# Parts of x for three batches and of LN's rows for two groups, made in token rows and transposed by DMA

## The chip, the cores and the metric

One core of a Trainium2 chip runs the whole program. The metric is the device time of one execution in microseconds; of the kernel before it is 833.95 us, the median of three runs (833.41 to 834.34). The engines go by these names: PE is TensorE (PEld its weight loads), DVE is VectorE, ACT is ScalarE, POOL is GpSimd, SP is SyncE, which here only issues DMAs.

## The reference

Three blocks in a row, all in f32: attention with a threshold, a LayerNorm with an MLP, and a token mixing with a channel product.

```python
scores = q @ k.T / sqrt(64)                 # 4 batches, 8 heads, 576 tokens
scores = where(scores >= max - tau, scores, -1e9)
x = softmax(scores) @ v                     # -> x: 4 x 576 x 512
xn = (x - mean) / sqrt(var + 1e-6) * g_ln
x = x + relu(xn @ w_ch1) @ w_ch2            # 512 -> 2048 -> 512
theta = x @ w_theta
y = w_tok_r @ (x*cos(theta)) + w_tok_i @ (x*sin(theta))   # over the tokens
u = x + y
out = u + relu(u @ w_ch)
```

## The kernel before

**Two parts for every operand.** The large products are made in fp16 with three products each: an f32 operand is scaled, rounded to fp16 (the rounded part, `hi`), and what is left of it is stored as a second fp16 (the difference, `lo`); rounded x rounded, rounded x difference and difference x rounded are added in PSUM.

**Who sets the order.** Nothing is ordered by hand. Each step is an `op(...)` with the operations it depends on, the buffers it acquires and releases (`Slot` of a `Res`) and a table of costs by engine (T for TensorE, A, V, G, Q for SP's queue). `Plan.run` plays the list several times, ranks the steps by their latest start and writes out one fixed order for each engine; TensorE goes by a `key`. A step with several engines in its table is given to the one that the plan sees finish first. A step that takes or frees another buffer can so move neighbours on all engines.

**Stages.** The attention runs to about 423 us, with LN and a first part of the MLP ("A") mixed in; the rest of the MLP ("B", products `p1_B...` and `c_...`) runs to about 630 us, and from 591 us on the token-mixing block goes batch by batch. Tokens come in row tiles of 128. Batches 0 and 1 are a pair of nine tiles, `xl_0_0` to `xl_0_8` (the tile in the middle, `xl_0_4`, holds 64 tokens of each batch and is called the tail), batches 2 and 3 a second pair, `xl_1_0` to `xl_1_8`. These tiles live in `x` slots and are loaded by SP from DRAM (L1349).

**LN.** For one row tile of a group (three tiles): `norm` writes the normalized rows `xn` in f32; `trans` (L1163) transposes them on TensorE, four blocks of 128 x 128 into PSUM; `hi` (L296 or L298, ScalarE or VectorE) rounds them from PSUM into `ringX`; `lo` (L309, VectorE) writes the difference. `ringX` then feeds the products of the MLP.

**The token-mixing block, for each batch b.**
- `scales` (L1457): TensorE makes `px_p` for the pair p from sums of squares; VectorE and GpSimd make a power of two of it (L619, L622, L625), the scale of x for theta, and small constants in `cs` (L1460 to L1475).
- `transposes(b)`, quoted below: the four transposes of a tile of x on TensorE (L1525, `pt3_...`), `hi` on ScalarE with the scale (L304), `lo` on VectorE (L1547), into `x1Tb`, which holds x transposed, rounded part and difference. The tail goes into a buffer of `hbuf`, and `tail1` and `tail2` copy its halves into the two batches' `x1T`.
- `thetas(b)`: 12 matmuls of 512 columns for a tile (L1573), then the reduction of theta on ScalarE, VectorE and GpSimd (L1591 to L1597).
- `make_z(b)`: sine, cosine (ScalarE), two products with x (L1660, VectorE), and the two parts of z (L298 to L309); the tail's are stacked first (L1694, L1695).
- `mix(b)`: y, 54 matmuls of 288 columns for each of four column blocks (L1737); the order of the rows of z ends with the tail's. Then u = x + y from PSUM (L1759), with the difference of x added (`post`, L1764, VectorE or GpSimd), and the parts of u written back over `x1Tb` (L304, L1770).
- `chan(b)`: o, 24 matmuls of 288 columns for each of four column blocks (L1795), each reading all four blocks of `x1Tb`; then relu, sum and the store.

`th_0` can only start when `x1T0` is there, `mix(0)` when all of z is. SP issues its DMAs in the order of its queue: one whose data are not ready holds up those behind it. The attention already turns its probabilities with DMA transposes on this queue (L1042, 108 of them, nine blocks of 128 x 128 each, `PT<-ringP`).

Of the kernel before, what the change touches and what calls it, by code (L numbers as in the profile page):

```python
# [75 lines left out]
MT = 2  # L76
IDLE = 200.0
NTINY = 960
BUSY = 0.7
LATE = 25000.0  # L80
CX = [0, 760.0, 1250.0]
CHA, CHV, CHG = [0, 680.0, 1160.0], [0, 690.0, 1290.0], [0, 758.0, 1370.0]
CLV, CLG = [0, 930.0, 1600.0], [0, 1206.0, 2060.0]
# [187 lines left out]
def tile_kernel(  # L271
# [45 lines left out]
    def vc(n, x=1.04):  # L317
        return 157.0 + x * n
# [10 lines left out]
    def gc(n):  # L329
        return 145.0 + GC * n  # L330
# [20 lines left out]
    rY = Res("y", 0)  # L351
    rXs = Res("x", NXS)
    rN = Res("xn", 2)
    rG = Res("g", 8)
    rR = Res("raw", NRAW)
    rQ, rK = Res("q", NQ), Res("k", NK)
# [102 lines left out]
    op(warmup, [k_ones], (warm,), (warm,), T=4000, key=-1e9)  # L459


    def cvt(src, shape, hi, lo, name, start=(), acq=(), kind="cvt", peak=None, late=None, early=False):


# [6 lines left out]
        def s0(e):  # L471
            if early:
                raw = rawe[sl.i // 2][:, sl.i % 2]
            else:
                raw = (lp if sl.i < NRAW else later["wb"]).tile([128, 512, 2], I32, tag=str(sl), name=f"raw_{name}")
# [626 lines left out]
    def ln_group(p, gi, base):  # L1102
# [44 lines left out]
        for t in range(nt):  # L1147
            sn, ms = Slot(rN), Slot(rM)

            def norm(e, t=t, sn=sn):  # L1150
                rs = st["rs"]
                st["xn", t] = lp.tile([128, S], F32, tag=str(sn), name=f"xn_{nm}_{t}")[:, 0:512]
                if e is A:
                    A.activation(out=st["xn", t], in_=x[p, t0 + t], func=AF.Identity,
                                 bias=rs[:, 1, t:t + 1], scale=rs[:, 0, t:t + 1])
                else:
                    V.tensor_scalar(out=st["xn", t], in0=x[p, t0 + t], scalar1=rs[:, 0, t:t + 1],
                                    scalar2=rs[:, 1, t:t + 1], op0=ALU.mult, op1=ALU.add)

            def trans(e, t=t, ms=ms):  # L1160
                st["pt", t] = m_tile(ms, [128, KB, 128], f"ptr_{nm}_{t}")
                for c in range(KB):
                    T.transpose(st["pt", t][:, c, :], st["xn", t][:, c * 128:(c + 1) * 128], ident)  # L1163

            def hi(e, t=t):
                st["xt"] = ringX[:, sx.i]
                copy(e, st["xt"][:, :, 0, t * 128:(t + 1) * 128], st["pt", t])

            def lo(e, t=t):
                cs = slice(t * 128, (t + 1) * 128)  # L1170
                sub(V, st["xt"][:, :, 1, cs], st["pt", t], st["xt"][:, :, 0, cs])

# [325 lines left out]
    def transposes(b):  # L1498
        p, odd = b // 2, b % 2
        sl = Slot(rY)  # L1500
        st = x1T[b] = {"sl": sl, "ops": [], "c": {}}
        t0 = 5 if odd else 0
        key = nkey() if b else KEY0

        def alloc():
            if "t" not in st:
                y = later["yp"].tile([128, KB, 2, S], F16, tag=str(sl), name=f"x1T{b}")
                st["t"] = [y[:, :, a] for a in range(2)]
            return st["t"]

        for t in range(5):
            if t == 4 and odd:
                def tail2(e):
                    for a in range(2):
                        copy(e, alloc()[a][:, :, 512:576], tails[p]["t"][:, :, a, 64:128])
                st["ops"].append(op(tail2, [tails[p]["op"]] + st["ops"][:1], (), (tails[p]["sl"],),
                                    A=2 * ac(256), V=2 * vc(256, .95)))
                continue
            ms = Slot(rM)
            ss = {}  # L1520

            def tr(e, t=t, ms=ms, ss=ss):
                ss["pt"] = m_tile(ms, [128, KB, 128], f"pt3_{b}_{t}")
                for c in range(KB):
                    T.transpose(ss["pt"][:, c, :], x[p, t0 + t][:, c * 128:(c + 1) * 128], ident)  # L1525

            acq = [ms]
            if t == 0:
                acq.append(sl)
            if t == 4:  # L1530
                tails[p] = {"sl": Slot(rG, 3)}
                acq.append(tails[p]["sl"])
            o = st["tr"] = op(tr, [xf[p, t0 + t], sx_ops[p], st.get("tr")], acq, (x_slot[p, t0 + t],), T=460, key=key + 0.01 * t)

            def dst(a, t=t):
                if t < 4:
                    return alloc()[a][:, :, t * 128:(t + 1) * 128]
# [12 lines left out]
            o = op(lo, [o], (), (ms,), V=690, kind="ev")  # L1550
            if t < 4:
                st["ops"].append(o)
            else:
                tails[p]["op"] = o

                def tail1(e):
                    for a in range(2):
                        copy(e, alloc()[a][:, :, 512:576], tails[p]["t"][:, :, a, 0:64])
# [363 lines left out]
```

## Time and profile before

| | us |
|---|---|
| median of 3 runs | 833.95 (833.41 to 834.34) |
| profiled execution | 833.26 |
| its span (first to last instruction) | 831.5 |
| PE busy | 821.0 (99%) |
| DVE busy | 621.0 (75%) |
| ACT busy | 535.0 (64%) |
| POOL busy | 355.8 (43%) |

The mean granted clock of TensorE is 0.999 of full speed. The span leaves out 1.8 us of the execution's own time, before the first and after the last instruction. Busy times are sums over an engine's instructions; they don't tell which engine is waited for at a given place, for that there are the rows of waits and of the timeline, where the idle time ahead of an instruction stands in square brackets with the instruction that ended it. A busy time in the timeline covers a matmul's drain, so the pace of matmuls is read from the start of one group to the start of the next.

### The profile page before, as it was taken

Reading aid. Unit: us, or ns where it says so; the run is one execution under the profiler, and the core shown is the slowest. Engines: PE = TensorE matmul, PEld = TensorE weight load, DVE = VectorE, ACT = ScalarE, POOL = GpSimd, SP = SyncE. Lnnn points to the kernel's source line nnn. Section 1 sums busy time; section 2 is a strip of 40 time slices with the busy share of each in tenths; the row PEclk is TensorE's granted clock in tenths of the full one; section 3 lists DMA queues with packets and bytes.
Section 4 is the critical chain, followed back from the end, with each engine's and each line's share of the span. In section 5 each row is a group of like instructions: output and inputs, shape, how many; then the busy total and the mean of one; then the engine's idle time right before and its main releaser. Section 6 shows DMA issues by size and latency. Waiting matters only on the chain. (4 is left out here: it accounts for less than half of the span.)

```text
span 831.5 us, 17300 instructions
## 1 busy us (share of the span) xinstructions
PE 821.0 (99%) x6625; PEld 543.4 (65%) x6625; DVE 621.0 (75%) x1279; ACT 535.0 (64%) x987; POOL 355.8 (43%) x444
## 2 busy tenths in 40 slices
PE   9999999999999999999999999999999999999997
PEld 8888866655566576666565555555555777667776
DVE  4878799999687887787557756766577693799943
ACT  5899999999588788888535543554476351564602
POOL 1332478787285465656321212221153250465611
PEclk9999999999999999999999999999999999999999
DMA  8433699894579799697563421744033010010011
GB/s 230 143 99 122 196 207 170 187 208 97 122 132 206 137 233 184 119 165 141 131 168 94 169 94 48 249 162 177 1 97 120 27 46 13 1 44 15 16 43 58
DMA packets 173235, 101.20 MB, mean 122 GB/s; under 512 B 136289, under 2 KB 154209, under 8 KB 173153
## 3 DMA queue, kind: packets, MB, share of 16 engines
q1 hardware_dynamic: 172864, 100.10, 49.5%
q8 instruction: 52, 0.85, 0.4%
q14 instruction: 31, 0.25, 0.1%
q10 hardware_dynamic: 288, 0.00, 0.0%
HBM read 52.50 MB, written 15.73 MB: 82 GB/s over the span
## 5 line engine op out<-in xcount | busy, mean ns | idle before, releaser
L701 PEld LDWEIGHTS <-w 128*128 128x128 f16 x1152 | 110.5, 98 | 80.7 <-issue 7.3
L701 PE MATMUL p_A<-ringX,w 128*128 128x384 f16 x864 | 149.9, 326 | 0.0
L724 PE MATMUL chA<-w,hbuf 128*128 128x512 f16 x648 | 149.2, 379 | 0.0
L724 PEld LDWEIGHTS <-hbuf 128*128 128x128 f16 x864 | 82.5, 99 | 93.6 <-issue 5.4
L979 DVE TENSOR_SCALAR_CACHE_REDUCE ringE<-S,ncoef 128x576 f32<-128x576 f32 x144 | 112.7, 812 | 27.2 <-PE S L878 21.1
L309 POOL TENSOR_TENSOR ringP<-ringE,ringP 128x512 f16<-128x512 f32 (+2 forms) x110 | 109.2, 1004 | 21.0 <-ACT ringP L296 16.1
L995 ACT ACTIVATE ringE<-ringE,tiny 128x576 f32<-128x576 f32 x144 | 105.5, 770 | 2.0 <-POOL tiny L987 1.0
L878 PE MATMUL S<-kf,qf 64*128 64x288 f32 (+1 forms) x576 | 98.5, 426 | 0.0
L1737 PE MATMUL y<-tok,z 128*128 128x288 f16 x768 | 97.2, 286 | 0.0
L1737 PEld LDWEIGHTS <-z 128*128 128x128 f16 x768 | 75.1, 98 | 19.2
L1021 ACT ACTIVATE ringE<-ringE,ntaup 128x576 f32<-128x576 f32 x108 | 78.6, 764 | 0.1
L707 ACT ACTIVATE hbuf<-p_A 128x384 f16<-128x384 f32 x72 | 35.2, 488 | 63.1 <-PE p_A L701 62.6
L878 PEld LDWEIGHTS S<-kf,qf 64*128 64x128 f32 (+1 forms) x576 | 56.9, 186 | 19.5 <-issue 4.5
L906 PEld LDWEIGHTS <-PT 128*128 128x128 f16 (+1 forms) x1680 | 57.3, 100 | 12.8 <-issue 5.4
L300 POOL TENSOR_SCALAR ringP<-ringE 128x576 f16<-128x576 f32 x63 | 44.7, 712 | 36.8 <-ACT ringE L1021 30.4
L906 PE MATMUL pv<-va,PT 128*128 128x65 f16 (+3 forms) x1680 | 60.2, 193 | 0.0
L1213 DVE SCALAR_TENSOR_TENSOR x<-chA,qs,x 128x512 f32<-128x512 f32 x54 | 40.3, 747 | 25.5 <-PE chA L724 25.3
L710 DVE SCALAR_TENSOR_TENSOR hbuf<-p_A,hbuf 128x384 f16<-128x384 f32 x72 | 39.6, 551 | 22.7 <-ACT hbuf L707 22.2
L724 PE MATMUL c<-w,hbuf 128*128 128x512 f16 x216 | 51.0, 379 | 0.0
L701 PE MATMUL p_B<-ringX,w 128*128 128x384 f16 x288 | 50.7, 326 | 0.0
L1795 PE MATMUL o<-x1T,cw 128*128 128x288 f16 x384 | 48.0, 286 | 1.3 <-DVE x1T L1770 1.3
L309 DVE TENSOR_TENSOR ringP<-ringE,ringP 128x512 f16<-128x512 f32 (+2 forms) x58 | 44.0, 768 | 2.9 <-ACT ringP L296 1.4
(228 smaller groups left out, 1392.8 us busy)
## 6 DMA issues: line engine op xcount, KB each, us to landing
raw_w<-in_w SPq DMA_DIRECT2D x20, 512.0 KB, 4.5
rawe<-in_w SPq DMA_DIRECT2D x12, 512.0 KB, 4.8
raw_tok<-in_wtok SPq DMA_DIRECT2D x12, 432.0 KB, 4.4
qf<-in_qT SPq DMA_DIRECT2D x20, 256.0 KB, 3.5
kf<-in_kT SPq DMA_DIRECT2D x16, 288.0 KB, 4.0
xscr<-x SPq DMA_DIRECT2D x18, 256.0 KB, 2.4
xl<-xscr SPq DMA_DIRECT2D x18, 256.0 KB, 5.1
out<-uo SPq DMA_DIRECT2D x16, 288.0 KB, 2.1
```

The lines of the kernel that those rows point to most:

```text
L300: G.tensor_scalar(out=out, in0=in_, scalar1=1.0, scalar2=0.0, op0=ALU.mult, op1=ALU.add)
L309: e.tensor_tensor(out=out, in0=a, in1=b, op=ALU.subtract)
L701: T.matmul(st["ps"][:, :n], lhsT=ch.w1(a, c), rhs=xt()[:, c, bb, :n], start=(kk == 0), stop=(kk == 11))
L724: T.matmul(ps, lhsT=h[:, a, t * 128:(t + 1) * 128], rhs=ch.w2(bb), start=(first and (a, bb) == M2[0]), stop=(stop and (a, bb) == M2[2]))
L878: T.matmul(w["S"][:, n, 0:288], lhsT=qd.q["f"][r, hp], rhs=d.k["f"][r, n * 288:(n + 1) * 288], start=True, stop=True)
L906: T.matmul(out[:, j * 65:j * 65 + n], lhsT=l, rhs=r[:, j * 65:j * 65 + n], start=(k == 0), stop=(k == len(seq) - 1))
L979: V.tensor_scalar(out=st["e"].rearrange("p (a k) -> p a k", a=2), in0=st["S"][:, :, 0:288], scalar1=ncoef, scalar2=None, op0=ALU.mult, op1 ...
L995: A.activation(out=st["e"], in_=st["e"], func=AF.Prelu, bias=cp["thr"][:, j:j + 1], scale=-1.0, alpha=STEEP)
L1021: A.activation(out=e_of(ws), in_=e_of(ws), func=AF.Exp, bias=ntaup, scale=1.0)
L1213: V.scalar_tensor_tensor(out=x[p, t0 + t], in0=st["ch", t], scalar=chunks[i].quad.inv, in1=x[p, t0 + t], op0=ALU.mult, op1=ALU.add)
L1737: T.matmul(st["ps"][n][:, 0:288], lhsT=a, rhs=w[:, n * 288:(n + 1) * 288], start=(k == 0 and q == 0), stop=(k == 8 and q == 2))
L1795: T.matmul(st["ps"][n][:, 0:288], lhsT=w[:, cs], rhs=d["t"][a][:, kk, n * 288:(n + 1) * 288], start=(kk == 0 and q == 0), stop=(kk == 3 an ...
```

## The change

For batches 0, 1 and 2 (`XQ`) and the LN groups (1,0) and (1,1) (`LNQ`), the transposes on TensorE go: 14 tiles of x (five, four, five) and six tiles of LN. Instead, for each tile, `hi_t` makes the scaled rounded part from the rows of x (or `xn`) in SBUF, in token rows (ScalarE, VectorE or GpSimd); `lo_t` makes the difference, also in token rows (VectorE; for LN GpSimd too); `turn_t` issues one DMA transpose on SP (8 blocks of 128 x 128, fp16) that writes both parts straight into `x1Tb`, the tail's `hbuf` buffer or `ringX`. The token rows of x take a slot of `raw` (x16 tiles), those of LN a new resource `x16` with two buffers. No PSUM buffer is used for these tiles. Batch 3 and the other LN groups stay as they were. `alloc()` returns the whole tile, and the copies of tails are rewritten to match.

```diff
+NX16 = 2
+LNQ = ((1, 0), (1, 1))
+XQ = (0, 1, 2)
...
+    rX16 = Res("x16", NX16)
...
+    def raw_tile(slot, name):
+        return (lp if slot.i < NRAW else later["wb"]).tile([128, 512, 2], I32, tag=str(slot), name=name)
...
+            def hi_t(e, t=t, parts=parts):
+                copy(e, parts()[:, :, 0, :], st["xn", t].rearrange("p (c k) -> p c k", c=KB))
+
+            def lo_t(e, t=t, parts=parts):
+                sub(e, parts()[:, :, 1, :], st["xn", t].rearrange("p (c k) -> p c k", c=KB), parts()[:, :, 0, :])
+
+            def turn_t(e, t=t, parts=parts):
+                st["xt"] = ringX[:, sx.i]
+                Q.dma_start_transpose(out=st["xt"][:, :, :, t * 128:(t + 1) * 128].rearrange("p c a k -> p (c a) k"),
+                                      in_=parts().rearrange("p c a k -> p (c a k)"))
...
+            if (p, gi) in LNQ:
+                o = first = op(norm, [o_rs, first], (sn,), A=808, V=vc(512, .95), kind="ln")
+                o = op(hi_t, [o], (s16,), A=ac(512), V=vc(512, .95), G=CHG[1] - 60.0, kind="lnev")
+                o = op(lo_t, [o], (), (sn,), V=vc(512, V2), G=gc(512), kind="lnev")
+                o = op(turn_t, [o] + xt[:1], () if xt else (sx,), (s16,), Q=1800, kind="lnev")
+                xt.append(o)
+                continue
...
+            def hi_t(e, parts=parts, xin=xin):
+                scopy(e, parts()[:, :, 0, :], xin(), px(p, X_S))
+
+            def lo_t(e, parts=parts, xin=xin):
+                V.scalar_tensor_tensor(out=parts()[:, :, 1, :], in0=xin(), scalar=px(p, X_S), in1=parts()[:, :, 0, :], op0=ALU.mult,
+                                       op1=ALU.subtract)
...
+            def turn_t(e, parts=parts, turned_=turned_):
+                Q.dma_start_transpose(out=turned_(), in_=parts().rearrange("p c a k -> p (c a k)"))
+
+            if b in XQ:
+                acq = [s16]
...
+                o = op(hi_t, [xf[p, t0 + t], sx_ops[p], st.get("hi")], acq, A=ac(512), V=vc(512, .95), G=CHG[1] - 60.0, kind="ev")
+                st["hi"] = o
+                o = op(lo_t, [o], (), (x_slot[p, t0 + t],), V=vc(512, V2), kind="ev")
+                o = op(turn_t, [o] + st["ops"][:1], (), (s16,), Q=1800, kind="ev")
+                if t < 4:
+                    st["ops"].append(o)
+                else:
+                    tails[p]["op"] = o
...
+                continue
```

The plan writes out a new order. On TensorE, at the place where batch 0's transposes stood (`pt3_0_...` are their PSUM tiles, `c_...` and `p1_B...` products of the MLP), the kernel before had:

```order
L724 LDWEIGHTS hbuf0_81
L724 MATMUL c_1_0_0_0_7579<-w2_12_6474,hbuf0_81 128x512
L1525 MATMUL pt3_0_0_7627<-ident_90,xl_0_0_7113 128x128 x4
L1525 MATMUL pt3_0_1_7634<-ident_90,xl_0_1_7123 128x128 x4
L1525 MATMUL pt3_0_2_7641<-ident_90,xl_0_2_7134 128x128 x4
L1525 MATMUL pt3_0_3_7650<-ident_90,xl_0_3_7257 128x128 x4
L724 LDWEIGHTS hbuf0_81
L724 MATMUL c_1_0_0_1_7585<-w2_12_6474,hbuf0_81 128x512
```

and the changed one comes to theta of batch 0 (`th_0_0`, weights `x1T0`) from a product of the MLP:

```order
L708 LDWEIGHTS w1_12_6272
L708 MATMUL p1_B1_1_0_7663<-ringX_80,w1_12_6272 128x384
L1657 LDWEIGHTS x1T0_7638
L1657 MATMUL th_0_0_7681<-th_6888,x1T0_7638 128x512
L1657 LDWEIGHTS x1T0_7638
```

The transposes are gone, and between `c_1_0_0_0` and `th_0_0` there now stand six matmuls for `c`, the product `p1_B1_0_3`, nine more for `c` and `p1_B1_1_0`, which followed theta of batch 0, or came in the midst of it, before.

On SP's queue, at the loads of the second pair's tiles (`xl_1_...<-xscr`) and the stores of finished tiles (`xfin<-xl_1_...`), before:

```order
L1349 DMA xl_0_8_7439<-xscr_110 128x512
L1363 DMA ringX_80<-scr11_109 128x3072
L1349 DMA xl_1_0_7548<-xscr_110 128x512
L1349 DMA xl_1_1_7555<-xscr_110 128x512
L1349 DMA xl_1_2_7782<-xscr_110 128x512
L1337 DMA xfin_111<-xl_1_0_7548 128x512
L1337 DMA xfin_111<-xl_1_1_7555 128x512
```

and after, with the DMA transposes out of the x16 tiles into `x1T0`, `x1T1` and the tail's `hbuf3`:

```order
L1382 DMA xl_1_0_7532<-xscr_110 128x512
L1382 DMA xl_1_1_7538<-xscr_110 128x512
L1579 DMA_TRANSPOSE x1T0_7638<-x16_0_0_7608 128x8x128
L1579 DMA_TRANSPOSE x1T1_7657<-x16_1_0_7614 128x8x128
L1579 DMA_TRANSPOSE x1T0_7638<-x16_0_1_7621 128x8x128
L1579 DMA_TRANSPOSE x1T0_7638<-x16_0_2_7630 128x8x128
L1579 DMA_TRANSPOSE x1T0_7638<-x16_0_3_7678 128x8x128
L1579 DMA_TRANSPOSE hbuf3_84<-x16_0_4_7696 128x8x128
L1370 DMA xfin_111<-xl_1_0_7532 128x512
L1370 DMA xfin_111<-xl_1_1_7538 128x512
L1579 DMA_TRANSPOSE x1T1_7657<-x16_1_1_7624 128x8x128
```

Six transposes stand right behind the load of `xl_1_1`, ahead of the first stores; the load of `xl_1_2`, which followed it directly, is now behind eight of them.

On VectorE, at the last products for z of batch 0 (`r_...` the sines, `co_...` the cosines, times `xl_0_...` and a constant of `cs`; `px_1` is the second pair's sum), before:

```order
L1660 SCALAR_TENSOR_TENSOR r_t0_7845<-xl_0_4_7268,cs_6164,r_t0_7845 128x512
L298 COPY x1T1_7968<-hbuf1_82 128x4x64 x2
L1547 SCALAR_TENSOR_TENSOR x1T1_7968<-pt3_1_3_7993,cs_6164,x1T1_7968 128x4x128
L619 TENSOR_SCALAR cs_6164<-px_1_8036 128x1
L1660 SCALAR_TENSOR_TENSOR co_0_tail_7979<-xl_0_4_7268,cs_6164,co_0_tail_7979 128x512
L1694 COPY r_t0_7845<-co_0_tail_7979 64x512
L1695 COPY r_t0_7845<-r_t0_7845 64x512
L1591 SCALAR_TENSOR_TENSOR r_1_0_8073<-t1_1_0_8052,cs_6164,th_1_0_8002 128x512
```

and after:

```order
L626 TENSOR_SCALAR cs_6128<-px_1_7975 128x1
L1744 SCALAR_TENSOR_TENSOR r_0_0_7724<-xl_0_3_7239,cs_6128,r_0_0_7724 128x512
L632 TENSOR_SCALAR cs_6128<-cs_6128 128x1
L1744 SCALAR_TENSOR_TENSOR co_0_3_7986<-xl_0_3_7239,cs_6128,co_0_3_7986 128x512
L1744 SCALAR_TENSOR_TENSOR r_t0_7956<-xl_0_4_7250,cs_6128,r_t0_7956 128x512
L1744 SCALAR_TENSOR_TENSOR co_0_tail_8002<-xl_0_4_7250,cs_6128,co_0_tail_8002 128x512
L1496 TENSOR_SCALAR cs_6128<-cs_6128 128x2
L1493 TENSOR_SCALAR cs_6128<-cs_6128 128x3
L1778 COPY r_t0_7956<-co_0_tail_8002 64x512
L1779 COPY r_t0_7956<-r_t0_7956 64x512
```

The read of `px_1` came behind the sine's product for the tail (`r_t0`) and now stands ahead of the last four products of batch 0's z; the differences of `x1T1` from `pt3_1_...` are gone from here.

## Rows read from the trace of the kernel before

**Rows 1.** Page, parts 1, 2: busy us (share) xinstructions; granted clock in tenths by slice.

```profile
PE 821.0 (99%) x6625; PEld 543.4 (65%) x6625; DVE 621.0 (75%) x1279; ACT 535.0 (64%) x987; POOL 355.8 (43%) x444
...
PEclk9999999999999999999999999999999999999999
```

**Rows 2.** Timeline, TensorE: start us, us, engine, line, operation, output<-inputs, shape, count.

```profile
591.03 1.91 PE L1525 MATMUL pt<-ident,xl 128*128 128x128 f32 x16
592.78 1.46 PE L724 MATMUL c<-w,hbuf 128*128 128x512 f16 x6
...
594.51 10.52 PE L1573 MATMUL th<-th,x1T 128*128 128x512 f16 x48
...
607.46 2.11 PE L701 MATMUL p_B<-ringX,w 128*128 128x384 f16 x12
609.41 2.11 PE L724 MATMUL c<-w,hbuf 128*128 128x512 f16 x9
```

**Rows 3.** TensorE's waits: waiting line <- releaser: us in total, times, longest.

```profile
PE pt L1525 <- DVE r_t L1591: 1.6, 1, 1.6
```

**Rows 4.** Timeline, TensorE, 372 to 374.

```profile
372.78 0.60 PE L1163 MATMUL ptr<-ident,xn 128*128 128x128 f32 x4
373.22 0.81 PE L724 MATMUL chA<-w,hbuf 128*128 128x512 f16 x3
```

**Rows 5.** Lines 304, 1547, 1660: duration ns min/median/max, first and last start.

```profile
L304 ACT ACTIVATE x1T<-pt,cs x16: 670/688/720, 591.7 to 741.4; 128x512 f16<-128x512 f32 x16
...
L1547 DVE SCALAR_TENSOR_TENSOR x1T<-pt,cs,x1T x16: 735/743/753, 592.4 to 743.2; 128x512 f16<-128x512 f32 x16
...
L1660 DVE SCALAR_TENSOR_TENSOR r<-xl,cs,r x16: 735/954/1772, 605.9 to 779.2; 128x512 f32<-128x512 f32 x16
```

**Rows 6.** Groups of instructions: busy us, mean ns | idle us before them, releasers.

```profile
L1764 DVE TENSOR_TENSOR u<-u,x1T 128x576 f32<-128x576 f32 x12 | 9.1, 756 | 0.3
...
L300 POOL TENSOR_SCALAR z<-co 128x512 f16<-128x512 f32 x3 | 2.7, 901 | 0.0
...
L1764 POOL TENSOR_TENSOR u<-u,x1T 128x576 f32<-128x576 f32 x4 | 6.3, 1588 | 34.2 <-DVE u L1759 34.2
```

**Rows 7.** Line 1042, the attention's DMA transposes on SP: as rows 5.

```profile
L1042 SPq DMA_TRANSPOSE PT<-ringP x108: 1242/1337/2912, 99.6 to 422.7; - x108
...
DMA to landing us min/median/max: 3.2/3.6/6.7
```

**Rows 8.** Timeline, VectorE, 589 to 592.

```profile
589.44 0.15 DVE L625 TENSOR_SCALAR cs<-cs 128x1 int32<-128x1 int32 x1 [0.66 <-POOL cs L622]
...
591.11 0.56 DVE L710 SCALAR_TENSOR_TENSOR hbuf<-p_B,hbuf 128x384 f16<-128x384 f32 x1 [1.06 <-ACT hbuf L707]
```

**Rows 9.** Timeline, SP, 577.

```profile
577.34 0.91 SPq L1349 DMA_DIRECT2D xl<-xscr  x2
```

**Rows 10.** Timeline, TensorE, 642 to 650.

```profile
642.90 6.04 PE L1737 MATMUL y<-tok,z 128*128 128x288 f16 x48
648.78 0.90 PE L1737 MATMUL y<-tok,hbuf 128*128 128x288 f16 x6
```

**Rows 11.** Timeline, VectorE and TensorE, 662 to 679 (idle before <-releaser).

```profile
662.82 0.94 DVE L1759 SCALAR_TENSOR_TENSOR u<-y,cs,x1T 128x288 f32<-128x288 f32 x2 [3.22 <-PE y L1737]
...
669.36 9.84 PE L1795 MATMUL o<-x1T,cw 128*128 128x288 f16 x79
...
676.56 1.71 DVE L1770 SCALAR_TENSOR_TENSOR x1T<-u,cs,x1T 128x576 f16<-128x576 f32 x1
```

**Rows 12.** Timeline, TensorE, 711 to 742.

```profile
711.23 10.52 PE L1573 MATMUL th<-th,x1T 128*128 128x512 f16 x48
...
740.74 0.66 PE L1525 MATMUL pt<-ident,xl 128*128 128x128 f32 x4 [1.56 <-DVE r_t L1591]
```

**Rows 13.** SP's own waits: as rows 3.

```profile
SPq L1042 <- POOL ringP L300: 28.9, 20, 4.9
```

**Rows 14.** Groups of instructions: weight loads of line 906.

```profile
L906 PEld LDWEIGHTS <-PT 128*128 128x128 f16 (+1 forms) x1680 | 57.3, 100 | 12.8 <-issue 5.4 <-DMA xscr<-x 0.4 <-DMA PT<-ringP 0.4
```

More of the change, by code (lines that the diff above doesn't have):

```diff
@@ L474, in s0 @@
             else:
-                raw = (lp if sl.i < NRAW else later["wb"]).tile([128, 512, 2], I32, tag=str(sl), name=f"raw_{name}")
+                raw = raw_tile(sl, f"raw_{name}")
             rw = st["rw"] = raw[:, 0:n, :]
@@ L1158, in norm, with parts @@
                                     scalar2=rs[:, 1, t:t + 1], op0=ALU.mult, op1=ALU.add)
+            s16 = Slot(rX16)
+            def parts(t=t, s16=s16):
+                if ("x16", t) not in st:
+                    st["x16", t] = ap.tile([128, KB, 2, 128], F16, tag=str(s16), name=f"xn16_{nm}_{t}")
+                return st["x16", t]
+            def hi_t(e, t=t, parts=parts):
[6 more added lines that the diff above has]
+                                      in_=parts().rearrange("p c a k -> p (c a k)"))
             def trans(e, t=t, ms=ms):
@@ L1506, in alloc @@
             if "t" not in st:
-                y = later["yp"].tile([128, KB, 2, S], F16, tag=str(sl), name=f"x1T{b}")
-                st["t"] = [y[:, :, a] for a in range(2)]
-            return st["t"]
+                st["y"] = later["yp"].tile([128, KB, 2, S], F16, tag=str(sl), name=f"x1T{b}")
+                st["t"] = [st["y"][:, :, a] for a in range(2)]
+            return st["y"]
         for t in range(5):
@@ L1514, in tail2, with parts @@
                     for a in range(2):
-                        copy(e, alloc()[a][:, :, 512:576], tails[p]["t"][:, :, a, 64:128])
+                        copy(e, alloc()[:, :, a, 512:576], tails[p]["t"][:, :, a, 64:128])
                 st["ops"].append(op(tail2, [tails[p]["op"]] + st["ops"][:1], (), (tails[p]["sl"],),
                                     A=2 * ac(256), V=2 * vc(256, .95)))
+                continue
+            s16 = Slot(rR)
+            ss = {}
+            def parts(ss=ss, s16=s16, t=t):
+                if "t" not in ss:
+                    ss["t"] = raw_tile(s16, f"x16_{b}_{t}").bitcast(F16).rearrange("p k two -> p (k two)")[:, 0:1024].rearrange(
+                            "p (c a k) -> p c a k", c=KB, a=2)
+                return ss["t"]
@@ new lines, in xin, with turned_ @@
+            def xin(t=t):
+                return x[p, t0 + t].rearrange("p (c k) -> p c k", c=KB)
+            def hi_t(e, parts=parts, xin=xin):
[3 more added lines that the diff above has]
+                                       op1=ALU.subtract)
+            def turned_(t=t):
+                if t < 4:
+                    return alloc()[:, :, :, t * 128:(t + 1) * 128].rearrange("p c a k -> p (c a) k")
+                i = tails[p]["sl"].i
+                tails[p]["t"] = hbuf[i // 2][:, i % 2].rearrange("p a n -> p (a n)").rearrange("p (c a k) -> p c a k", c=KB, a=2)
+                return tails[p]["t"].rearrange("p c a k -> p (c a) k")
@@ new lines, in turn_t, with tail1 @@
+            def turn_t(e, parts=parts, turned_=turned_):
+                Q.dma_start_transpose(out=turned_(), in_=parts().rearrange("p c a k -> p (c a k)"))
+            if b in XQ:
+                acq = [s16]
+                if t == 0:
+                    acq.append(sl)
+                if t == 4:
+                    tails[p] = {"sl": Slot(rG, 3)}
+                    acq.append(tails[p]["sl"])
+                o = op(hi_t, [xf[p, t0 + t], sx_ops[p], st.get("hi")], acq, A=ac(512), V=vc(512, .95), G=CHG[1] - 60.0, kind="ev")
+                st["hi"] = o
+                o = op(lo_t, [o], (), (x_slot[p, t0 + t],), V=vc(512, V2), kind="ev")
+                o = op(turn_t, [o] + st["ops"][:1], (), (s16,), Q=1800, kind="ev")
+                if t < 4:
+                    st["ops"].append(o)
+                else:
+                    tails[p]["op"] = o
+                    def tail1(e):
+                        for a in range(2):
+                            copy(e, alloc()[:, :, a, 512:576], tails[p]["t"][:, :, a, 0:64])
+                    st["ops"].append(op(tail1, [o] + st["ops"][:1], (), (tails[p]["sl"],), A=2 * ac(256), V=2 * vc(256, .95)))
@@ L1536, in dst @@
                 if t < 4:
-                    return alloc()[a][:, :, t * 128:(t + 1) * 128]
+                    return alloc()[:, :, a, t * 128:(t + 1) * 128]
                 if "t" not in tails[p]:
@@ L1557, in tail1 @@
                     for a in range(2):
-                        copy(e, alloc()[a][:, :, 512:576], tails[p]["t"][:, :, a, 0:64])
+                        copy(e, alloc()[:, :, a, 512:576], tails[p]["t"][:, :, a, 0:64])
                 st["ops"].append(op(tail1, [o] + st["ops"][:1], (), (tails[p]["sl"],), A=2 * ac(256), V=2 * vc(256, .95)))
```

## The prediction

> **What bounds the kernel now.** I read the page's busy table first, then who waited for whom on TensorE, then its timeline where the transposes stand, then the other engines there. TensorE is busy 821.0 of 831.5 us and holds its full granted clock in every slice [rows 1]. An "always busy" engine could still hide stalls, so I checked the steps: 12 matmuls of 384 columns take 609.41 - 607.46 = 1.95 us, 60 theta matmuls of 512 columns 607.46 - 594.51 = 12.95 us (0.216 each), with nothing between the pieces [rows 2]. The waits that TensorE shows are few, the longest 1.6 us at a transpose of x [rows 3]. So the sum of TensorE's instructions sets the time in almost every stage, and what leaves TensorE is gained unless a new wait replaces it.
>
> **What leaves TensorE.** Twenty row tiles lose their four transposes: batch 0 five, batch 1 four, batch 2 five, and six tiles of LN. Price of a tile: sixteen transposes (four tiles) run from 591.03 to 592.78, 1.75 us, so 0.437 each [rows 2]. LN's are the same, 372.78 to 373.22 [rows 4]. Sum: 20 x 0.437 = 8.74 us. Some cost up to 0.50 where they break up other work (up to 0.06 more on six, 0.4 us at most).
>
> **What is added, and what hides it.**
> Element work stays at two operations a tile: a rounded part, then the difference. The rounded part took ScalarE 0.69 us from PSUM; now it is made from SBUF on ScalarE, VectorE or GpSimd, for which GpSimd's 0.90 is the nearest row [rows 6]. The difference took VectorE 0.743 us with almost no spread, one input being the PSUM tile. Now both inputs lie in SBUF, and the nearest row, a product of that kind at line 1660, spreads from 0.735 to 1.77 [rows 5]. So 20 x 0 to 1 us more element work, on engines that are 75%, 64% and 43% busy [rows 1], off TensorE's path as long as each tile has cover. The Trainium skill, page "SBUF — State Buffer", section "Who interferes with whom", says that a VectorE instruction with two SBUF inputs contends with a GpSimd instruction that reads SBUF, and one with a single SBUF input does not. The two spreads fit it; by that rule the new differences are the slow kind whenever GpSimd is at work.
>
> A DMA transpose of nine blocks holds SP's queue 1.34 us (1.24 to 2.91) and lands after 3.6 us (3.2 to 6.7) [rows 7]. I take the same for the new ones of eight blocks. The Trainium skill, page "VectorE: DVE Perf Modes", sections "The three transpose paths" and "Rules for kernel authors", advises TensorE for 128x128 where a PSUM destination will do, at 390 ns against 1309 ns by DMA for one bf16 block. Taken as a serial price this would be 8 x 1.3 = 10.5 us a tile, some 90 us for the nine tiles of batches 0 and 1, and the change a large loss. The trace disagrees: nine blocks land within 3.6 us.
>
> *Batches 0 and 1.* Theta of batch 0 no longer follows its transposes directly; the order puts MLP work ahead of it. From the point where the transposes stood (591.03) there run 6 + 9 matmuls of 512 (0.216 each, so 1.30 + 1.95 us) and twice 12 of 384 (3.90), so th_0_0 comes at 598.2. Is its DMA there? The scale px is ready by 589.6, and VectorE's piece of the MLP that stands ahead ends at 591.7 [rows 8]; the rounded part lies beside it, and the difference (0.74 to 1.77) ends at 592.4 to 593.5; plus 3.6 makes 596.0 to 597.1. Cover 1.1 to 2.2 us at the usual landing, a stall of up to 2.0 at the longest landing. Later tiles follow every 1.34 us on SP, and theta takes 2.59 a tile, so the first is the tightest. On SP the transposes stand behind the loads xl_1_0 and xl_1_1, which went out at 577.34 at once [rows 9]; the third such load, which needs a free x slot, now stands behind them. I cost the landing at nothing.
>
> The price of the move is less time for z of batch 0. th_t0 ends at 598.2 + 2.59 + 1.95 + 4 x 2.59 = 613.1 instead of 607.46, while the token mixing starts 9 x 0.437 = 3.93 us earlier, at 638.97 instead of 642.90, and reads the tail's z last, 48 matmuls or 648.78 - 642.90 = 5.88 later: 644.85 [rows 10]. VectorE now waits for px_1 first, which TensorE ends 5.83 us before mixing (2.25 theta tiles), at 633.1. Behind it on VectorE, by the new order, are four products (4 x 0.74 to 1.77 [rows 5]), two copies (at most 0.74 each), eight small scale operations of 0.15 with a wait of 0.66 for GpSimd between them, as with px_0 [rows 8], then ScalarE's part (0.69) and the difference (0.74 to 1.77): 7.8 to 12.9 us, ready between 640.9 and 646.0. Just in time: I cost it at nothing, at worst 646.0 - 644.85 = 1.2.
>
> *Into the channel product.* After y_0_3 the product o_0 needs the fourth column block of x1T0. Before, that block took 676.56 + 1.71 - 669.36 = 8.9 us, and TensorE had 72 matmuls of 288 (5.88 / 48 = 0.1225 each [rows 10]) ahead of it, 8.8 us [rows 11]: already on the edge. In the new order 60 stand ahead, 7.35 us, and the sum u_0_3 goes to GpSimd (1.59 there, against 0.76 on VectorE [rows 6]). VectorE's own queue there, two adds (0.94), three products, one sum, the difference, is 4.7 us at the fast rates and 9.0 at the slow. With 8.0, nearer the 8.9 that is measured here, the stall is 0.7 us (0 to 1.7). This is the one loss I put in.
>
> *Batch 2.* Its element work moves into the mixing of batch 1, where VectorE has waits like the 3.22 us for y [rows 11], over 10 us before it is needed: free. Theta starts 2.2 us earlier against the mixing. The stall of 1.56 us ended at 740.74, 29.5 us after theta's start; the new order has there theta (12.95), 120 matmuls of 288 (14.7) and three tiles of batch 3's transposes (1.3), 28.95 us [rows 12]: 0.6 us of stall remains, 1.0 gained. VectorE also takes two sums from GpSimd there, so I count 0 (1.0 gain to 1 loss).
>
> *LN groups.* Their transposed parts are read, by the order, some 900 TensorE instructions later; no direct wait. Six DMA transposes are slid between the attention's own on SP. Counted at nothing; at worst one product of the attention waits by as much as the longest landing is over the usual, 6.7 - 3.6 = 3.1 us [rows 7].
>
> **Sum.** 833.26 (the profiled execution) - 8.74 + 0.7 = 825.2; this execution lies 0.7 us under the median, 833.95, so 825.9.
>
> **Rivals.** *A: VectorE sets the pace from the mixing of batch 0 on.* Its block of x1T0 came just when TensorE needed it [rows 11]. If that moment is fixed by VectorE's work, the 3.93 us of batches 0 and 1 are given back there in place of the 0.7: 825.9 + 3.2 = 829.1. Against it: just before, VectorE itself waited 3.22 us for y [rows 11], so it follows TensorE.
> *B, the other side: the attention starves.* SP takes DMAs in order. An LN transpose waits there for its difference, now mostly on GpSimd behind the attention's own pieces; the attention's transposes behind it are late, and TensorE, in a fixed order, waits for PT. SP's longest wait for such a GpSimd piece is 4.9 us [rows 13]; with 1.34 for the instruction, 6.2. It decides from 1.34 us of uncovered wait for each of the six (8.04 / 6). Two of the six without cover give 12.5: 825.9 + 12.5 = 838.4, slower. For it: the queue is dense there. Against it: over all 108 transposes TensorE's weight loads waited 0.4 us for PT [rows 14], so there is cover.
>
> **How the numbers follow.** The forecast 0.74, A 0.13, B 0.07; 0.06 for A with half of B, which ends near no change. What a measurement here can tell is about 0.2%, 1.7 us (beyond 832.3 or 835.6): faster 0.87, within 0.06, slower 0.07. The range takes in the bounds: down 0.7 (no stall into the channel product), 1.0 (batch 2) and 0.4 (LN) to about 823.5; up the ends are 1.2 (z), 1.0 (o_0), 1.0 (batch 2) and 3.1 (the attention), 6.3 in all; as they hardly fall together I take 5.1 of it, to 831.0, which holds A as well.
>
> **What would show it.** TensorE's busy time falls to about 812, with no transposes of batches 0 to 2; theta of batch 0 starts without a wait; TensorE's waits list o_0 for VectorE's x1T with less than 2 us, and no DMA. Wrong would be: theta waiting for a DMA (landings over 5 us), o_0 or y waiting several us for VectorE (A), or pv waiting for PT between 300 and 420 us (B).

## The result and the profile after

The changed kernel takes 822.63 us (median of 4 runs, 822.16 to 823.12), the kernel before, beside it, 833.68: a ratio of 0.987, with a 95% interval of 0.985 to 0.988. It is faster by 11.05 us, where 8.0 had been forecast (825.9, range 823.5 to 831.0): the direction is right, the size too small, and the time lies 0.9 us below the range.

Busy times and clock of the page after, for [rows 1]:

```profile
PE 812.1 (99%) x6545; PEld 534.8 (65%) x6545; DVE 616.6 (75%) x1271; ACT 536.0 (65%) x990; POOL 369.9 (45%) x449
...
PEclk9999999999999999999999999999999999999999
```

TensorE is busy 8.9 us less, close to the 8.74 us of transposes; the other engines' sums hardly moved (GpSimd 14 us more). But the span fell by 831.5 - 820.6 = 10.9 us, so some 2 us are not transposes but waits that went. The waits on TensorE for which [rows 3] has the longest of before (waiting line, releaser: total, times, longest):

```profile
PE o L1879 <- DVE x1T L1854: 0.6, 1, 0.6
PE pt L1609 <- DVE r_t L1675: 0.2, 1, 0.2
```

The wait at batch 3's last transpose (`pt` for `r_t`) was 1.6 and is 0.2. The wait at `o` stood at 1.3 in the kernel before, and 0.6 now, but these are two different places, as the timelines show. TensorE after (start, us, line, operation, shape, count, idle time before and what ended it):

```profile
584.12 2.07 PE L1490 MATMUL px<-cs,ones 128*128 128x1 f32 x18
...
595.78 2.75 PE L1657 MATMUL th<-th,x1T 128*128 128x512 f16 x12
...
636.57 6.04 PE L1821 MATMUL y<-tok,z 128*128 128x288 f16 x48
...
663.03 7.76 PE L1879 MATMUL o<-x1T,cw 128*128 128x288 f16 x62
671.41 4.32 PE L1879 MATMUL o<-x1T,cw 128*128 128x288 f16 x34 [0.62 <-DVE x1T L1854]
675.57 6.04 PE L1821 MATMUL y<-tok,z 128*128 128x288 f16 x48
...
702.03 10.52 PE L1657 MATMUL th<-th,x1T 128*128 128x512 f16 x48
...
731.38 0.66 PE L1609 MATMUL pt<-ident,xl 128*128 128x128 f32 x4 [0.23 <-DVE r_t L1675]
...
765.76 11.92 PE L1879 MATMUL o<-x1T,cw 128*128 128x288 f16 x96
777.52 6.04 PE L1821 MATMUL y<-tok,z 128*128 128x288 f16 x48
```

and the rows of before that stand beside them, as far as [rows 2, 10 to 12] don't have them:

```profile
586.51 2.06 PE L1457 MATMUL px<-cs,ones 128*128 128x1 f32 x18
...
681.12 6.04 PE L1737 MATMUL y<-tok,z 128*128 128x288 f16 x48
...
707.58 1.91 PE L1525 MATMUL pt<-ident,xl 128*128 128x128 f32 x16
...
775.27 7.76 PE L1795 MATMUL o<-x1T,cw 128*128 128x288 f16 x62
784.36 4.33 PE L1795 MATMUL o<-x1T,cw 128*128 128x288 f16 x34 [1.32 <-DVE x1T L1770]
788.52 6.04 PE L1737 MATMUL y<-tok,z 128*128 128x288 f16 x48
```

Read from start to start, this places the whole difference:

| stretch on TensorE | before | after | difference | forecast |
|---|---|---|---|---|
| start to px_0 (attention, LN) | 586.51 | 584.12 | -2.39 | -2.62 |
| px_0 to y_0 (batches 0, 1) | 56.39 | 52.45 | -3.94 | -3.93 |
| o_0 | 11.76 | 12.54 | +0.78 | +0.7 |
| end of y_1 to o_2 (batch 2, theta of 3) | 67.69 | 63.73 | -3.96 | -2.19 |
| o_2 | 13.25 | 11.76 | -1.49 | 0 |
| from then on | 42.98 | 43.08 | +0.10 | 0 |

The stretches left out, y_0 and y_1, take 26.46 us in both. The three terms that the forecast worked out most closely came within 0.25 us; what it missed is 1.77 us between y_1 and o_2 beyond five transposes, and 1.49 us in o_2, 3.26 us together. For the profiled execution the forecast was 825.2; it took 822.35, 2.85 less, which is these 3.26 less the 0.4 that the other terms gave back.

The DMA side did as costed. Duration (ns, min/median/max) and landing of the new transposes, and the new differences on VectorE:

```profile
L1579 SPq DMA_TRANSPOSE x1T<-x x12: 1232/1290/2058, 590.2 to 685.0; - x12
...
DMA to landing us min/median/max: 3.0/3.3/4.7
```

```profile
L1568 DVE SCALAR_TENSOR_TENSOR x<-xl,cs,x x14: 734/737/973, 589.2 to 681.8; 128x512 f16<-128x512 f32 x14
```

They land after 3.3 us, theta of batch 0 starts at 595.78 without a wait, and the differences take 0.737 us, at most 0.97: the fast end of the bounds, not the slow one.

### The profile page after: what moved, and what is told of

Its sections match the earlier page's. It is cut to its first block, busy times and chain, and to the rows that moved or that the text cites. A ratio compares the mean times of both kernels' runs of the same rounds, so it can differ in the third digit from the quotient of the medians.

```text
span 820.6 us, 17207 instructions
## 1 busy us (share of the span) xinstructions
PE 812.1 (99%) x6545; PEld 534.8 (65%) x6545; DVE 616.6 (75%) x1271; ACT 536.0 (65%) x990; POOL 369.9 (45%) x449
## 4 chain that ended last, share of the span: by engine, by line
PE 93%; DVE 3%; ACT 2%; issue 1%; POOL 0%; DVEq 0%; POOLq 0%; ACTq 0%
PE chA L731 17%; PE p_A L708 17%; PE y L1821 11%; PE S L885 11%; PE pv L913 6%; PE p_B L708 6%; PE c L731 6%; PE th L1657 5%; PE pv L900 5%; PE o L1879 4%; PE tm L957 2%; PE warm L453 1%; PE th_t L1657 1%; DVE r L1744 1%; PE ptr L1188 1%
## 5 line engine op out<-in xcount | busy, mean ns | idle before, releaser
L312 POOL TENSOR_TENSOR ringP<-ringE,ringP 128x512 f16<-128x512 f32 (+2 forms) x112 | 112.8, 1018 | 27.7 <-ACT ringP L299 24.8
L303 POOL TENSOR_SCALAR ringP<-ringE 128x576 f16<-128x576 f32 x58 | 42.0, 727 | 30.7 <-ACT ringE L1028 26.3
```

## The experiments

The error has two candidate causes. **Order**: the two waits went because TensorE's work around theta of batch 2 was put in another order, in particular 12 matmuls of o_1 that stood ahead of theta and now stand behind it. **Relief**: each tile that leaves PSUM and VectorE takes some of the waits with it, wherever it was. Beneath both is the question why VectorE was late at those places at all.

**Parts of the change.** Three kernels differ from the changed one by one or two numbers:

```diff
-LNQ = ((1, 0), (1, 1))      # x_only
+LNQ = ()
...
-XQ = (0, 1, 2)              # ln_only
+XQ = ()
...
-XQ = (0, 1, 2)              # x01_ln
+XQ = (0, 1)
```

> Only the 14 tiles of x are turned by DMA (LNQ empty). Order theory (TensorE's sum sets the time; the stalls at the last transpose of batch 3 and at o_2 went because TensorE's work around theta of batch 2 was put in another order): 14 x 0.437 = 6.1 us of transposes, the two stalls of 1.75 and 1.49 us (by the starts of the pieces) gone, 0.78 us of new stall at o_0: 833.7 - 6.1 - 1.75 - 1.49 + 0.78 = 825.1. Relief theory (each tile that leaves PSUM and VectorE takes a bit off the stalls, so LN's tiles have a share): above 825.6, with the two stalls partly back.

> Only the six LN tiles (XQ empty). Order theory: 6 x 0.437 = 2.6 us less, or 2.4 as the start of px_0 moved in the trace of the changed kernel; both stalls stay at 1.6 and 1.3 us: 831.1 to 831.3. Relief theory: the same or less, with smaller stalls. If the LN transposes starved the attention: above 832.

> Batch 2 back on TensorE, the rest as in the change. TensorE's order from y_1_3 to o_2 is again that of the kernel before. Order theory: both stalls are back (1.6 at the last transpose of batch 3, about 1.3 at o_2), five transposes of 0.437 too: 833.7 - 6.33 + 0.78 = 828.1. Relief theory: the nine tiles of batches 0 and 1 and LN's six relieve the later stages too, stalls well under 1 us each: 825 to 826.5.

Measured: x_only 825.74 us (0.990 of before, 0.988 to 0.991), ln_only 831.60 (0.997, 0.9955 to 0.998), x01_ln 828.75 (0.994, 0.992 to 0.995). The six LN tiles bring 833.93 - 831.60 = 2.3 us, 0.3 less than their 2.62, and the time lies 0.3 above the order theory's band; the attention doesn't starve. With batch 2 back on TensorE (x01_ln) the wait at `pt` is 1.6 again and the one at o_2 1.3, to the tenth, though 15 of the 20 tiles are still gone: relief falls. By its median, x_only lies where the relief theory put it (above 825.6), and x01_ln 0.65 above the order theory's 828.1; the timelines decide, not the medians. In x_only the wait at `pt` is 0.2 and o_2 takes 11.76 us, without a wait, so neither stall is partly back. From px_0 on it needs 235.7 us against 236.5 for the changed kernel, because the new stall of 0.78 at o_0, which its forecast had in the sum, isn't there either (o_0 takes 11.76). Its loss lies in the attention, where the plan settled, from early on, on another order than in the kernel before and in the changed one.

**Only the 12 matmuls put back.** In the changed kernel the first two steps of o_1's second column block get a key ahead of theta of batch 2:

```diff
-                       key=key + 0.01 * c)
+                       key=key - 1.5 if (b, c) == (1, 1) and kk < 2 else key + 0.01 * c)
```

> The change, with the first 12 matmuls of o_1 for its second column block put ahead of theta of batch 2 again, where the kernel before had them; nothing else is asked for. Order theory: theta starts 12 x 0.1225 = 1.47 us later, the chain from theta to r_t (29.3 to 29.4 us in both traces) ends later by as much, and the stall at the last transpose of batch 3 goes from 0.2 to about 1.7 us: 822.6 + 1.5 = 824.1. Relief theory: the stall stays at 0.2, 822.6.

Measured: 825.96 us (825.35 to 827.05), 3.3 more than the changed kernel, where 1.5 or 0 had been expected. TensorE's waits and its timeline there:

```profile
PE o L1879 <- DVE x1T L1854: 1.9, 2, 1.3
PE pt L1609 <- DVE r_t L1675: 1.6, 1, 1.6
```

```profile
702.55 1.63 PE L1879 MATMUL o<-x1T,cw 128*128 128x288 f16 x12
704.02 10.52 PE L1657 MATMUL th<-th,x1T 128*128 128x512 f16 x48
...
733.53 0.66 PE L1609 MATMUL pt<-ident,xl 128*128 128x128 f32 x4 [1.56 <-DVE r_t L1675]
...
768.07 7.76 PE L1879 MATMUL o<-x1T,cw 128*128 128x288 f16 x62
777.15 4.33 PE L1879 MATMUL o<-x1T,cw 128*128 128x288 f16 x34 [1.32 <-DVE x1T L1854]
781.32 6.04 PE L1821 MATMUL y<-tok,z 128*128 128x288 f16 x48
```

Both waits are back at their old size, 1.56 and 1.32 us. By the starts, y_1's end to o_2 takes 768.07 - 702.55 = 65.52, 1.79 more than in the changed kernel, and o_2 13.25, 1.49 more: 3.28 us, all of the 3.26 that the forecast missed, from the order alone. It is the order of all engines: with the 12 matmuls the plan also moved y_2 a little (24 of its matmuls instead of 30 ahead of theta of batch 3, as in the kernel before), gave the two sums `uo` of batch 1 that VectorE had back to GpSimd, and listed VectorE's work at o_2 in another order. The first half was expected (theta starts 1.47 later, and r_t, which ends 29.45 us behind theta's start in the kernel before, 29.30 in the changed one and 29.46 here, with it). That o_2 follows was not.

**Why VectorE is late.** At o_2 the last block of x1T is the last thing that VectorE owes. Kernel before, VectorE and GpSimd:

```profile
781.91 1.78 POOL L1808 TENSOR_TENSOR uo<-x1T 128x576 f32<-128x576 f16 x1
782.48 1.82 DVE L1770 SCALAR_TENSOR_TENSOR x1T<-u,cs,x1T 128x576 f16<-128x576 f32 x1
```

changed kernel:

```profile
770.18 1.72 POOL L1892 TENSOR_TENSOR uo<-x1T 128x576 f32<-128x576 f16 x1
...
772.37 0.80 DVE L1854 SCALAR_TENSOR_TENSOR x1T<-u,cs,x1T 128x576 f16<-128x576 f32 x1
...
773.18 1.61 POOL L312 TENSOR_TENSOR z<-co,z 128x512 f16<-128x512 f32 x1 [1.29 <-ACT z L299]
```

The same instruction takes 1.82 us beside GpSimd's sum and 0.80 in a gap of GpSimd. It ends 9.03 us after o_2's start in the kernel before and 7.41 in the changed one, and the 62 matmuls ahead of the place of the wait take 7.6; 1.02 of the 1.62 us between them is its own duration, the rest lies in VectorE's work ahead of it. To test that this is a cause, GpSimd is kept from reading: where it has a difference of z or a sum `uo`, it writes zeros, so that this part of the result is missing. The planner's tables are unchanged, so the orders of all engines stay.

```diff
-                        sub(e, st["z"][:, j, 1, :], st[w], st["z"][:, j, 0, :])
+                        if e is G:
+                            G.memset(st["z"][:, j, 1, :], 0.0)
+                        else:
+                            sub(e, st["z"][:, j, 1, :], st[w], st["z"][:, j, 0, :])
...
-                e.tensor_tensor(out=st["u"][:, 0], in0=d["t"][0][:, c, :], in1=d["t"][1][:, c, :], op=ALU.add)
+                if e is G:
+                    G.memset(st["u"][:, 0], 0.0)
+                else:
+                    e.tensor_tensor(out=st["u"][:, 0], in0=d["t"][0][:, c, :], in1=d["t"][1][:, c, :], op=ALU.add)
```

> The kernel before, where GpSimd, for its share of z's differences and of the sums ahead of the result, writes zeros instead of reading and computing (that part of the result is left out); all orders stay. If VectorE's slow instructions (1.6 to 1.8 us instead of 0.7 to 0.8) come from GpSimd reading beside them, they become fast, the last block of x1T for o_2 (1.82 us, ending 9.0 us after o_2's start) comes 1.5 us or more earlier and the stall of 1.3 us goes; the chain to r_t of batch 2, with three slow z differences in it, shortens too: 830.7 to 832.3. If the slow form has another cause: 833.7 and both stalls as before.

> The same in the changed kernel (the same part of the result left out). If GpSimd's reading causes the slow form: the stall of 0.6 us at o_0 goes (0.78 by the starts of the pieces), and 0.2 at the last transpose of batch 3: 821.6 to 822.0, and VectorE's last block for o_0 takes 0.8 instead of 1.71 us. Otherwise 822.6.

Measured: gset_before 829.97 us (829.56 to 830.32), 3.7 less than the kernel before; gset_after 821.30 (820.87 to 821.60), 1.3 less than the changed one. Both lie below the bands for the contention, by 0.7 and 0.3: the effect is larger than expected. In gset_before both waits are gone, and the other stretches from px_0 on are as before to 0.05 us; TensorE:

```profile
739.29 0.60 PE L1525 MATMUL pt<-ident,xl 128*128 128x128 f32 x4
...
773.61 11.92 PE L1798 MATMUL o<-x1T,cw 128*128 128x288 f16 x96
785.37 6.04 PE L1740 MATMUL y<-tok,z 128*128 128x288 f16 x48
```

and the block of x1T, duration of the 16 (ns, min/median/max), kernel before and gset_before:

```profile
L1770 DVE SCALAR_TENSOR_TENSOR x1T<-u,cs,x1T x16: 805/819/1821, 654.1 to 817.6; 128x576 f16<-128x576 f32 x16
```

```profile
L1773 DVE SCALAR_TENSOR_TENSOR x1T<-u,cs,x1T x16: 798/817/902, 654.7 to 814.5; 128x576 f16<-128x576 f32 x16
```

The slow form of this instruction, up to 1.82 us, is absent: 0.90 at most. The block for o_2 runs beside a GpSimd that writes, and stays fast:

```profile
777.87 1.00 POOL L1682 MEMSET z<- 128x512 f16 x2
778.23 0.80 DVE L1773 SCALAR_TENSOR_TENSOR x1T<-u,cs,x1T 128x576 f16<-128x576 f32 x1
```

So the block that TensorE waits for was slow because GpSimd read SBUF beside it, and so was the work on the way to r_t: beside a difference of z and the four sums of batch 1 on GpSimd, three differences of z and two of the last sums take VectorE 8.07 us in the kernel before (1.64, 3.44 and 2.99 from 725.66 on), and 2.90 in gset_before (0.68, 1.28 and 0.94).

**Both edits together** tell whether the order does harm by itself or only through these slow instructions:

> The change with both edits: 12 matmuls of o_1 ahead of theta of batch 2 again, and GpSimd writing zeros for its share of z's differences and of the sums ahead of the result (that part of the result left out). With the first edit alone the time rose by 3.3 us, to 825.96, through two stalls (1.6 at the last transpose of batch 3, 1.3 at o_2). If the order does harm only through VectorE's slow instructions beside a reading GpSimd, both stalls are gone and the time is that of the second edit alone, 821.3, within 0.4. If the order itself costs (theta starts 1.47 us later, and its chain sets the moment), 822.3 or more, with the stall at batch 3's last transpose left.

Measured: 821.81 us (821.12 to 822.08), 0.1 above the band for the first case and 0.5 below the second. The timeline decides:

```profile
702.27 1.63 PE L1882 MATMUL o<-x1T,cw 128*128 128x288 f16 x12
...
731.23 0.60 PE L1609 MATMUL pt<-ident,xl 128*128 128x128 f32 x4
...
765.55 11.92 PE L1882 MATMUL o<-x1T,cw 128*128 128x288 f16 x96
777.31 6.04 PE L1824 MATMUL y<-tok,z 128*128 128x288 f16 x48
```

No wait at either place. y_1's end to o_2 takes 63.28 us, in gset_after 63.27 (701.70 to 764.97), and o_2 11.76 in both; the 0.5 between the medians lies ahead of px_0 (585.13 against 584.56 in the profiled executions). So the old order costs 3.3 us while GpSimd reads beside VectorE, and nothing between y_1 and the end of o_2 when it doesn't.

**The landing that was costed at nothing.** Each DMA transpose is issued a second time, first into the same place, then into a spare buffer:

```diff
-                Q.dma_start_transpose(out=turned_(), in_=parts().rearrange("p c a k -> p (c a k)"))
+                for _ in range(2):                                        # turn_twice
+                    Q.dma_start_transpose(out=turned_(), in_=parts().rearrange("p c a k -> p (c a k)"))
...
+                spare[0] += 1                                             # turn_spare, behind the first
+                Q.dma_start_transpose(out=spare[1][:, 0], in_=parts().rearrange("p c a k -> p (c a k)"))
```

> The change, with each of its 20 DMA transposes issued twice, one right behind the other. The forecast's cover for theta of batch 0 was 1.1 to 2.2 us, in the trace of the change about 2.3; one more instruction of 1.3 us fits in: 822.6 to 823.0. On SP six of them cost the attention's queue 6 x 1.34 = 8.0 us; if that queue has no slack (rival B), pv waits for PT by several us and the time is 825 or more.

> The change, with a second DMA transpose behind each of the 20, out of the same rows into a spare buffer that nobody reads. In the run with two transposes into the same place the second waited for the first one's landing, so a pair held SP's queue for 4.5 us and the time rose by 28 us. Here only the spare buffer is waited for, by the next tile's second transpose: a pair should hold the queue 2.7 to 3.5 us. Theta of batch 0 takes 2.59 us a tile and had 2.3 us of cover in the changed kernel: it falls behind by up to 1 us a tile, a wait of 0 to 3 us there; the attention's queue is held 6 x 1.34 = 8 us longer by LN's. If both have slack (the forecast's zero was right with room): 822.6 to 824. If SP's queue has none: 830 or more, with waits for PT.

Measured: turn_twice 850.96 us, turn_spare 829.84 (829.23 to 831.36). The first was badly made. The second write into the same place waits for the first one's landing, so that a pair holds the queue for 22.31 / 5 = 4.46 us:

```profile
595.32 22.31 SPq L1581 DMA_TRANSPOSE x1T<-x  x10
```

It says that this is far too much: the pairs of LN, 4.4 to 5.4 us each, bring px_0 to 589.24, 5.1 us later, and theta of batch 0 waits for DMAs in four places. turn_spare lies 7.2 us above the changed kernel, past the 822.6 to 824 that slack would have given and just under the 830 for no slack, and where the loss lies is instructive. px_0 starts at 583.96, against 584.12: six more transposes on SP cost the attention nothing. Theta of batch 0 waits 0.2 us for its fourth tile and 0.7 for the tail; th_t starts 1.0 us later than in the changed kernel. The rest is one wait on TensorE with what follows on it, and behind it one on VectorE (TensorE's waits, its timeline, VectorE's waits):

```profile
PE th_t L1662 <- DMA hbuf<-x: 0.7, 1, 0.7
```

```profile
622.58 3.46 PE L732 MATMUL c<-w,hbuf 128*128 128x512 f16 x8 [4.65 <-DVE hbuf L718]
```

```profile
DVE xl L1366 <- DMA xl<-xscr: 5.3, 1, 5.3
```

SP at that moment:

```profile
614.72 1.30 SPq L1582 DMA_TRANSPOSE x1T<-x  x1
616.65 1.23 SPq L1584 DMA_TRANSPOSE spare<-x  x1
617.99 1.47 SPq L1385 DMA_DIRECT2D xl<-xscr  x3
```

VectorE's next instruction adds to the tile xl_1_2, whose load stands on SP behind the transposes of batches 0 and 1 and goes out at 617.99, where the changed kernel sends it at 603.84. VectorE waits 5.3 us for it with the MLP's difference `hbuf` behind it in its queue, and TensorE waits for that. The transposes' own data had room; the load behind them was sent 14.15 us later and missed by 5.3, so it had about 9 us. The wait cost more than its length: the eight matmuls behind it take 3.30 us from start to start (622.58 to 625.88) where eight took 1.73 in the kernel before (0.216 each). The granted clock of TensorE, 1.00 ahead of the idle 4.65 us, is 0.50 from 622.58 to 625.5 (1.2 GHz, the lower of its two levels), and 1.00 again from 626 on. So this one wait is worth some 6.2 us.

**Batch 3 as well.**

```diff
-XQ = (0, 1, 2)
+XQ = (0, 1, 2, 3)
```

> Batch 3 turned by DMA as well. Order theory: four more tiles leave TensorE, 1.75 us, and the last stall of 0.2 to 0.45 with them, as no PSUM buffer is waited for: 820.4 to 820.7. Rival: with all of it on VectorE's side theta of batch 3 or z of batch 2 waits for VectorE instead: 822 or more, with a wait at th or y.

Measured: 825.12 us (824.69 to 826.15), 2.5 more than the changed kernel: the rival's place and size, though what ends the wait is a DMA. Of the 2.3 us between the profiled executions, 0.9 lies ahead of px_0 (585.06 against 584.12) and was not traced; 1.4 lies behind it. SP and TensorE at theta of batch 3:

```profile
732.64 1.23 SPq L1579 DMA_TRANSPOSE x1T<-x  x1
...
735.79 1.47 PE L1657 MATMUL th<-th,x1T 128*128 128x512 f16 x6 [3.54 <-DMA x1T<-x]
```

There are two buffers for x1T, so that batch 3's takes the one of batch 1, and its first part is made only after o_1 has read it, at 728.57. The rounded part is done at 729.30, VectorE comes to the difference only at 731.75, behind other work, the transpose goes out at 732.64, and TensorE starts 3.15 us later, after a wait of 3.54 us. So VectorE's load has a share of 2.45 us in the delay, and the landing the larger one; with transposes on TensorE the same step is two operations from PSUM. A DMA has room here only where the buffer is free early.

**GpSimd without z's differences**, everything computed; and without the sums too:

```diff
-                    done.append(op(lo, [o], (), [sl], V=vc(512, V2), G=gc(512)))
+                    done.append(op(lo, [o], (), [sl], V=vc(512, V2)))
...
-            o_p = op(pre, [o_pre, d["c"][c]], [sn], V=vc(576, V2), G=gc(576), kind="ev")     # noG_both
+            o_p = op(pre, [o_pre, d["c"][c]], [sn], V=vc(576, V2), kind="ev")
```

> The change, with the differences of z on VectorE alone (GpSimd not offered to the plan); everything is computed. VectorE gets some 18 differences more at 0.69 us, but fewer of its own instructions are slow. If GpSimd's reading costs VectorE more than it takes off it: 821.3 to 822.3, stalls at o_0 and at batch 3's last transpose below 0.2. If VectorE's own load decides: 823.5 or more, with stalls at o for x1T.

> As the run before it, with the sums ahead of the result on VectorE alone as well (16 sums of 576 columns at 0.75 us). If contention decides: 821.2 to 822.3. If VectorE's load decides: later than the run before it, above 823.5.

Measured: noG_z 821.52 us (821.25 to 822.31), the fastest of the kernels that compute everything, 1.1 under the changed one; but against the kernel before, each beside its own runs of it, the ratios are 0.985 (0.9835 to 0.987) and 0.987 (0.985 to 0.988), intervals that overlap. The waits at o_0 and at batch 3's last transpose are gone, and one of 0.3 us at o_2 is there. noG_both takes 823.88 (823.50 to 824.33), by its number the case of VectorE's load, but from px_0 on both need 235.7 us; its loss lies in the attention, where the plan took x_only's order up to LN's tiles, with waits that the changed kernel doesn't have there:

```profile
PE pv L913 <- DMA PT<-ringP: 0.9, 1, 0.9
PE pv L913 <- DVE tiny L588: 0.9, 1, 0.9
```

So VectorE can carry both alone (but for differences of the tails, two of which stayed on GpSimd), and the verdict on noG_both is about the plan, not about the sums.

## Why the prediction was right and wrong

*TensorE sets the time, and a tile is worth 0.437 us.* Right. Batches 0 and 1 gave 3.94 us for nine tiles (3.93 forecast), LN 2.39 for six (2.62), batch 2 2.19 for five, as gset_before and gset_after show, where TensorE waits nowhere between y_1 and o_2 (65.46 - 63.27). What ate 0.23 us of LN's in the attention was not traced further.

*Element work at no cost, landing at nothing.* Right. The Trainium skill, page "SBUF — State Buffer", section "Who interferes with whom", led me to expect the new differences in their slow form beside GpSimd; here the measurement differs: beside GpSimd's rounded parts, which read SBUF (587.30 to 592.25), none of them took over 0.97 us, and the median is 0.737. The same rule, that GpSimd's reads and not its writes disturb a VectorE instruction with two SBUF inputs, is what gset_before shows on the block of x1T (1.82 us beside a GpSimd that reads, 0.80 beside one that writes).

*The stall of 0.7 us into o_0.* Right to 0.1: 0.78 by the starts, one slow block (1.71 us) among slow neighbours. Two small errors cancel in it: the block ends 8.3 us after o_0's start, where 8.0 was taken, and 62 matmuls stand ahead of the wait, where 60 were counted.

*Batch 2: counted as 0.* This step failed. Its own working gave 1.0 us of gain (28.95 us of work on TensorE against 29.5 for VectorE's chain) and I then set it to 0 because two sums moved to VectorE. The measured gain is 1.77: the wait fell from 1.56 to 0.23, and the pauses around the single tiles of batch 3's transposes shrank too. By the starts TensorE lost 2.0 us between theta and that last transpose before, of which the wait is 1.56, and 0.4 after, where the working had 0.6: what it had too small was the loss of before. With the two sums on VectorE the chain from theta to r_t took 29.30 us against 29.45, so they cost nothing there. Theta starts 3.65 us earlier against the mixing, not 2.2: the 12 matmuls of o_1 (1.47) left the place ahead of it as well.

*o_2: not in the sum at all.* This is the larger omission in kind. A wait of 1.3 us stood in the list of TensorE's waits of before, at `o`. I took it as staying, without asking which block of o it was and what stood ahead of it. It was VectorE's slow form that made it, as in o_0 (gset_before, where o_2 takes 11.76 us instead of 13.25); and I had used just that pair of rates, fast and slow, to forecast a new stall at o_0, without noticing that the same reordering could take one away. A forecast that lets reordering create a stall has to let it remove one.

*Range.* Its lower end allowed 0.7 + 1.0 + 0.4 us of luck, which from 825.9 makes 823.8 and not the 823.5 that was written, and the time lies 0.9 below even that, for want of the 1.5 us at o_2.

*Rivals.* A (VectorE fixes the moment of o_0) is out: y_0 to o_0 moved with TensorE's start, 26.46 us in both. B (the attention starves) is out with a factor of two to spare: px_0 in turn_spare is no later with twice the LN transposes on SP; at 4.4 to 5.4 us a pair, in turn_twice, it is 5.1 us later. A risk that the forecast named and gave no price, the load of xl_1_2 behind the transposes, is the one that turn_spare brought out.

## What to carry to other kernels

List every wait of the bounding engine with its place and its cause before counting a change's work, and ask of each whether the new order keeps it: here waits of 1.6 and 1.3 us were worth more than a third of the transposes. Where VectorE's duration for one instruction has two values, find who reads SBUF beside it; such an instruction on the critical path is a reason to try the stage without GpSimd, and its slow value can come and go with a change of order elsewhere, as at o_0 and o_2 here. When transposes go to a DMA queue, price the loads and stores behind them and the moment at which the destination is free, not the DMA alone.

## What was not expected of the hardware

- A second DMA transpose into the same place, which waits for the first, holds the queue 4.46 us a pair; into a spare buffer, which the pair before it has to have filled, a pair holds it some 3.3.
- After 4.65 us without work (turn_spare) TensorE's granted clock was 0.50 for the next 3 us, and eight matmuls took 1.6 us longer than eight at 1.00.
- GpSimd made a scaled rounded part in 1.74 us, twice the 0.90 of the nearest row of before, where ScalarE took 0.71:

```profile
L309 POOL TENSOR_SCALAR x<-xl,cs 128x512 f16<-128x512 f32 x4 | 7.0, 1744 | 0.3 <-DVE cs L632 0.3
```

  The first of them ran before VectorE's first new difference, so that contention with it doesn't explain them all; no run here separates the cause. It cost no time.
- Two kernels got another attention order from the planner though they differ from a neighbour only far behind the attention: x_only from the kernel before (px_0 3.2 us later in the profiled executions, of which x_only's is itself 1.4 above its median) and noG_both from the changed one (1.9 later). A comparison of such kernels has to be read stage by stage.
